# Row maxima of attention scores by key differences: half of the evictions moved to ScalarE, the rest fused on VectorE

## The chip, the cores and the metric

One Trainium2 chip; the kernel runs on one of its cores. The metric is device microseconds of one execution, the median of several. Engines: PE is TensorE (matmuls), PEld its weight loads, DVE is VectorE, ACT is ScalarE, POOL is GpSimd, SP is SyncE, which here only issues transfers.

## The reference

Three stages in a row: attention with pooled queries, a soft mixture of experts, and a two-layer network with a quadratic step.

```python
# q, k, v: (4, 8, 1152, 64); the queries are averaged in pairs
q_pool = q.reshape(B, H, S // 2, 2, D).mean(axis=3)            # 576 queries
scores = scale * q_pool @ k.transpose(0, 1, 3, 2)              # 576 x 1152 for each of 32 heads
scores = scores - np.max(scores, axis=-1, keepdims=True)       # the row maxima
attn = np.exp(scores); attn = attn / (attn.sum(-1, keepdims=True) + 1e-9)
x = (attn @ v).transpose(0, 2, 1, 3).reshape(2304, 512)
# mixture: logits = x @ phi (32 slots), softmax over tokens, two layers for each expert,
#          then softmax over slots and back to 2304 x 512
# network: h = x @ w_in; g = h if h >= 1, 0 if h <= -1, else (h + 1)**2 / 4; out = g @ w_out
```

## The kernel before

**Attention, two heads at a time.** There are 16 pairs of heads (`P`), and for each pair 9 chunks of 128 keys (`c`), so 144 steps `g = 9 P + c`. Each step has two halves, one for each head (`h`). In a half, TensorE works in this order: a part of the row maxima of a later pair (`max_half`), the transposed scores of this step (`st`), and the product of the step before with the values (`pv`). The maxima run `LEAD = 11` steps ahead of the scores that use them, so pair 0's maxima come in a lead-in before step 0, and pair 1's are pressed into steps 0 to 6 (`P1G`), two of them in each of the steps 0 and 1.

**Row maxima.** For each of 9 groups `t` of 128 queries (from both heads) the products with all 1152 keys are formed, in two parts `a` of 2 x 288 keys. `K1` holds the keys in fp16 as a rounded part and its remainder, one below the other on the partitions, and `q1` the rounded queries twice, so that one matmul gives both products. Each part goes to a PSUM buffer of the ring `sc` (3 buffers, tag `sc`), and VectorE takes the maximum over its 576 columns (L332), into `mp[P][:, t, a]`. For three groups at a time of pair 0 (`RT`), ScalarE copies the first part to fp16 instead (L327), and VectorE takes the maxima of the copies in halves (`max_rt`, L342). `max_fin` takes the larger of the two columns and puts it, scaled, beside the queries' remainder in `qn2`; that tile is transposed into `q2`. The scores are then a second matmul with `q2` and `S2`, whose rows hold the rounded keys and a constant row for the maximum: the maximum is subtracted in the matmul.

**The ring.** Score tiles (`st`), maxima tiles and the tiles of `t_x` share the 3 buffers of `sc`. A maxima tile reuses the buffer of the score tile two halves before, and a score tile that of the maxima tile one half before: a late eviction holds up TensorE.

**After the scores.** ScalarE takes the exp of a score tile (L407) into `E`, a ring of 4 + 3 SBUF buffers (`e`, `e2`). The sums over keys are made by first adding tiles: VectorE adds chunks 1, 2, 3 and 5 to chunk 0 (`es_add`, L415, by the list `ADD`), after GpSimd has added chunk 4 into 3 and 7 into 6 (`ge_add`, L420, by `GAD`). Then matmuls with a column of ones sum over the partitions (`es_sum`, L430), one block of matmuls for each group of `GRP`: before, three blocks (the added-up tile, 6 with 7, and 8).

**Between pairs.** At step 0 of the next pair TensorE does a transposing product for the pair before the last one (`t_x`, L479) and the row sums (`es_sum`); ScalarE copies results (`t_raw` L448, `t_sum` L456, `t_ev` L483) and scales tokens (`t_mul` L492, at places from the list `TML`); VectorE makes the divisors (`t_fin`, L460 to L464). Every fourth pair a softmax over the tokens of a batch is added.

**The order of the work is written out by hand.** `at(g, slot, f)` puts a call into a half-step; the lists `PREP` (loads, rounding and transposes of a later pair's keys and queries: `prep_khi`, `prep_klo`, `prep_qp`, `prep_qhi`, `prep_qlo`, `xpose_k`, `xpose_q1`), `CVS` and `CVL` (places of the weight conversion) hold such places. In a half-step's slot the calls come behind the matmuls of that half. All transfers are issued by SyncE, in program order.

**Weight conversion.** Sixteen pieces of the last layer's weights are loaded as pairs of 32-bit words and turned into floats: `cv_load`, `cv_abs` (ScalarE, L203), four `cv_step` (VectorE, L210 to L218), `cv_move` (to DRAM). Before, eleven pieces run in pairs 1 to 14, four steps each at step 0, and five in pair 15. The rest of the weights is converted in the last stage.

**Behind attention** come the mixture (weights of 1 MB each, loaded ahead piece by piece) and the network, whose matmuls (L1050) fill the last 220 us. The change doesn't touch their work.

Of the kernel before, what the change touches and what calls it, by code (L numbers as in the profile page):

```python
# [11 lines left out]
I32 = mybir.dt.int32  # L12
# [8 lines left out]
FILL = 38, 2, 8, 5  # L21
# [13 lines left out]
ADD = (((4, 1, 0, 0, 2), (6, 1, 1, 0, 2), (7, 2, 0, 0, 2), (8, 2, 1, 0, 2), (11, 3, 0, 0, 2), (12, 3, 1, 0, 2),  # L35
        (14, 5, 0, 0, 2), (15, 5, 1, 0, 2)),
       tuple((2 * c + h + 2, c, h, 0, 2) for c in range(1, 7) for h in range(2)))

PREP = (-20, -18, (-34, -33), -36, -16, -30), (-24, -21, (-36, -35), -37, -17, -31)
# [3 lines left out]
def fused_kernel(ctx: ExitStack, tc: tile.TileContext, q, k, v, phi, w1, w2, w_in, w_out, out):  # L43
# [60 lines left out]
    f64b = [cst([128, DM, 2], f"f64_{i}", I32) for i in range(2)]  # L104
# [76 lines left out]
    sq = xf[:, 1952:1952 + 2 * SW]  # L181

# [123 lines left out]
    def s2_fill(P):  # L306
        nc.sync.dma_start(out=S2b[P % 2][0:64], in_=K1[P][0:64])

    def max_half(P, t, a):
        if t == 0 and a == 0:  # L310
            mp[P] = g2.tile([128, NK, 2], F32, tag="mp", name=f"mp{P}")
# [12 lines left out]
        rt = RT[P] if P < len(RT) else ()  # L324
        if rt and a == 0 and rt[0] <= t < rt[-1]:

            nc.scalar.activation(out=mcp[:, t].rearrange("p (i n) -> p i n", i=2), in_=ps[:, :, 0:HQ], func=AF.Copy,  # L327
                                 scale=1.0 / MS)
            if t + 1 in rt:
                max_rt(P, rt[rt.index(t + 1) - 1], t + 1)  # L330
            return
        nc.vector.tensor_reduce(out=mp[P][:, t, a:a + 1], in_=ps[:, :, 0:HQ], op=ALU.max, axis=AX.XY)  # L332
        if mc:
            mc.pop(0)()

    mc = []
    mcp = xl.bitcast(F16)[:, 0:NK * TQ].rearrange("p (t n) -> p t n", t=NK)

    def max_rt(P, t0, t1):
        x, n, o = mcp[:, t0:t1], HQ, mp[P][:, t0:t1, 0]  # L340
        while n > HQ // 8:
# [872 lines left out]
```

## Time and profile before

| | |
|---|---|
| median of 3 runs | 739.67 us (738.88 to 740.59) |
| the profiled execution | 738.26 us, span 736.5 us |
| TensorE busy | 720.2 us, 98% of the span |
| VectorE busy | 587.4 us, 80% |
| ScalarE busy | 462.5 us, 63% |
| GpSimd busy | 221.4 us, 30% |
| granted TensorE clock | 1.00 throughout |

The span is what the profile covers, and the run's own time has 1.8 us around it. Times in rows are microseconds from the span's start unless marked ns. "idle before <-X" says how long the engine had been idle and what ended that.

### The profile page before, as it was taken

The page shows a single profiled execution, that of the slowest core. Times are in us where ns is not written, and L with a number is a line of the kernel's source. Part 1 is how long each engine was busy: PE and PEld are TensorE (multiplying, and loading weights), DVE is VectorE, ACT ScalarE, POOL GpSimd, SP SyncE. Part 2 cuts the span into 40 slices and gives each one's busy share as a digit, 9 for nine tenths or more (in the row PEclk, how much of TensorE's full clock was granted, in tenths as well). Part 3 has the DMA queues.
Part 4 walks back from the last instruction along what each step waited for, and adds up shares of the span by engine and source line. Part 5 has one row for each costly group of instructions (what it writes and reads, how often), then busy time and mean ns, then how long its engine had stood idle before and what let it go on. Part 6 is the DMA issues. An engine that isn't in the chain of part 4 may idle for free.

```text
span 736.5 us, 19455 instructions
## 1 busy us (share of the span) xinstructions
PE 720.2 (98%) x8017; PEld 563.8 (77%) x8017; DVE 587.4 (80%) x993; ACT 462.5 (63%) x881; POOL 221.4 (30%) x197
## 2 busy tenths in 40 slices
PE   8799999999999999999999999999999999999998
PEld 8677787877787877777877776536888888888887
DVE  5999999989999989999989758524667898896552
ACT  4355667757667757667766668314797677667640
POOL 6221132132132232232232232012533244424350
PEclk9999999999999999999999999999999999999999
DMA  9699789886878986877975619897102121200122
GB/s 211 147 226 222 164 204 214 189 195 148 163 216 196 189 204 143 191 198 187 200 189 132 217 35 294 323 416 312 58 1 86 61 83 58 87 28 1 72 86 101
DMA packets 130649, 118.75 MB, mean 161 GB/s; under 512 B 81152, under 2 KB 99840, under 8 KB 128512
## 3 DMA queue, kind: packets, MB, share of 16 engines
q1 hardware_dynamic: 130560, 117.50, 60.1%
q8 instruction: 63, 1.03, 0.6%
q14 instruction: 26, 0.21, 0.1%
HBM read 82.90 MB, written 8.91 MB: 125 GB/s over the span
## 4 chain that ended last, share of the span: by engine, by line
PE 86%; DVE 7%; issue 3%; DMA 2%; ACT 2%; SPq 0%; DVEq 0%; ACTq 0%
PE po L1050 26%; PE st L402 18%; PE acc L437 16%; PE mx L318 8%; PE tx L479 4%; PE acc L430 3%; DVE mp L332 3%; PE h L980 2%; PE s2o L851 2%; PE h L794 2%; DVE es L415 1%; ACT e L407 1%; DMA f<-in_moe_w_out_dram 1%; PE po L1056 1%; DMA kf<-in_k_dram 1%
## 5 line engine op out<-in xcount | busy, mean ns | idle before, releaser
L407 ACT ACTIVATE e<-st 128x576 f32<-128x576 f32 x288 | 187.5, 651 | 101.9 <-PE st L402 95.5
L332 DVE TENSOR_REDUCE mp<-mx 128x1 f32<-128x576 f32 x282 | 210.3, 748 | 27.9 <-PE mx L318 24.7
L437 PE MATMUL acc<-e,vf 128*64 128x288 f32 x1152 | 198.9, 408 | 1.7 <-ACT e L407 1.7
L402 PE MATMUL st<-q,K 128*64 128x288 f16 x1152 | 128.5, 288 | 3.9 <-DVE mp L332 2.4
L318 PE MATMUL mx<-K,q 128*64 128x288 f16 x1152 | 124.2, 286 | 4.8 <-DVE mp L332 2.7
L402 PE MATMUL st<-q,S 128*64 128x288 f16 x1152 | 128.5, 286 | 0.0
L420 POOL TENSOR_TENSOR e<-e,e 128x576 f32<-128x576 f32 x60 | 88.7, 1499 | 132.4 <-PE acc L437 126.2
L318 PEld LDWEIGHTS <-q 128*64 128x64 f16 x1152 | 76.1, 110 | 55.3 <-issue 6.0
L1019 POOL TENSOR_TENSOR glo<-r,ghi 128x1024 fp32r<-128x1024 f32 x34 | 81.9, 2408 | 114.5 <-DVE r L1007 74.2
L1050 PE MATMUL po<-whi,ghi 128*128 128x512 f32 x280 | 109.8, 392 | 0.0
L1050 PE MATMUL po<-wlo,ghi 128*128 128x512 f32 x280 | 109.6, 391 | 0.0
L1050 PE MATMUL po<-whi,glo 128*128 128x512 f32 x280 | 109.4, 391 | 0.0
L402 PEld LDWEIGHTS <-K 128*64 128x64 f16 x1152 | 74.2, 109 | 24.2 <-issue 13.1
L437 PEld LDWEIGHTS acc<-e,vf 128*64 128x64 f32 x1152 | 82.2, 137 | 8.3 <-issue 4.0
L415 DVE TENSOR_TENSOR es<-es,e 128x576 f32<-128x576 f32 x100 | 84.2, 843 | 0.0
L402 PEld LDWEIGHTS <-S 128*64 128x64 f16 x1152 | 75.6, 110 | 1.0 <-issue 0.2
L1062 DVE TENSOR_TENSOR pa<-po,pa 128x512 f32<-128x512 f32 (+1 forms) x54 | 36.8, 681 | 39.8 <-PE po L1050 39.7
L1050 PEld LDWEIGHTS po<-whi,glo 128*128 128x128 f32 x280 | 52.6, 188 | 12.0 <-POOL glo L1019 0.3
L1050 PEld LDWEIGHTS po<-whi,ghi 128*128 128x128 f32 x280 | 52.6, 188 | 10.9 <-issue 0.4
L1050 PEld LDWEIGHTS po<-wlo,ghi 128*128 128x128 f32 x280 | 52.6, 188 | 10.1
L1007 DVE SCALAR_TENSOR_TENSOR r<-h,cl 128x512 f32<-128x512 f32 x68 | 43.6, 681 | 7.6 <-ACT cl L1003 4.1
L492 ACT ACTIVATE xl<-xl,ss 128x96 f32<-128x96 f32 x150 | 47.1, 366 | 0.0
(204 smaller groups left out, 877.6 us busy)
## 6 DMA issues: line engine op xcount, KB each, us to landing
w<-in_moe_w_dram SPq DMA_DIRECT2D x76, 256.0 KB, 4.0
w<-in_moe_w_dram SPq DMA_DIRECT2D x12, 1024.0 KB, 12.3
vf<-in_v_dram SPq DMA_DIRECT2D x16, 576.0 KB, 4.2
kf<-in_k_dram SPq DMA_DIRECT2D x30, 288.0 KB, 5.0
f<-in_moe_w_in_dram SPq DMA_DIRECT2D x16, 512.0 KB, 4.9
f<-in_moe_w_out_dram SPq DMA_DIRECT2D x16, 512.0 KB, 3.5
qf<-in_q_dram SPq DMA_DIRECT2D x30, 256.0 KB, 5.8
S<-K SPq DMA_DIRECT2D x16, 288.0 KB, 4.6
```

Source lines behind the costliest of these rows:

```text
L318: nc.tensor.matmul(ps[p0:p1, i, 0:HQ], lhsT=q1[P][:, t, p0:p1], rhs=kk[:, j * HQ:(j + 1) * HQ], start=True, stop=True)
L332: nc.vector.tensor_reduce(out=mp[P][:, t, a:a + 1], in_=ps[:, :, 0:HQ], op=ALU.max, axis=AX.XY)
L402: nc.tensor.matmul(ps[c0:c0 + 64, i, 0:HQ], lhsT=kk[:, ci, c0:c0 + 64], rhs=f[:, sl[i]], start=first, stop=not first)
L407: nc.scalar.activation(out=e, in_=ps[:, :, 0:HQ], func=AF.Exp, scale=ESC)
L415: nc.vector.tensor_tensor(out=Es[P, n, h][:, i0:i1], in0=a[:, i0:i1], in1=b[:, i0:i1], op=ALU.add)
L420: nc.gpsimd.tensor_tensor(out=E[P, c, h], in0=E[P, c, h], in1=E[P, c + 1, h], op=ALU.add)
L437: nc.tensor.matmul(acc[P, i][h * 64:(h + 1) * 64, 0:HQ], lhsT=vt[P][:, h, c, :], rhs=E[P, c, h][:, i, :], start=(c == 0), stop=(c == NK - ...
L492: nc.scalar.activation(out=x, in_=x, func=AF.Copy, scale=ss[P][:, h, t:t + 1])
L1007: nc.vector.scalar_tensor_tensor(out=r[:, a:a + 2], in0=ps[a // 2], scalar=-1.0, in1=cl[:, a:a + 2], op0=ALU.max, op1=ALU.add)
L1019: nc.gpsimd.tensor_tensor(out=glo[k], in0=r, in1=ghi[k].bitcast(F32), op=ALU.subtract)
L1050: nc.tensor.matmul(ps, lhsT=a, rhs=b, start=st_, stop=sp)
L1062: nc.vector.tensor_tensor(out=t, in0=po, in1=t, op=ALU.add)
```

## The change

The maximum of two products a and b is a + max(b - a, 0). The changed kernel uses it for the two halves of a head's keys. VectorE forms the differences of the keys once a pair (`k_diff`: second half less first half, in fp16, into `KD`). The first part of each group's maxima is then the product with the differences; ScalarE evicts it as its positive part (Relu) into `RW`, an SBUF tile with two buffers. The second part is the product with the first half of the keys; VectorE adds the positive parts to it and takes the maximum in the same instruction (`tensor_tensor_reduce`), straight into `mp`. The matmuls stay as many. The copies of pair 0 (`RT`, `max_rt`) and the small maximum in `max_fin` are gone. Around that:

- GpSimd's adds (`ge_add`) are gone; VectorE adds chunks 1 to 7 to chunk 0 (14 adds a pair instead of 8), and there are two blocks of row sums in a pair instead of three, but for the last pair, which is as before. The ring `e2` has 4 buffers instead of 3.
- The weight conversion runs at one piece a pair, at fixed places, and each load is issued behind the piece before it, into one buffer instead of two.
- There is one `S2` instead of two, filled in two parts: chunks 0 to 4 four steps before the pair, the others at its step 0.
- The places of the preparation (`PREP`), of `t_mul` (`TML`) and of the adds are new; `prep_qhi`, for one, moves from the pair's step 1 to step 0. Pair 0 has fewer fill matmuls (`FILL`).

```diff
-FILL = 38, 2, 8, 5
+FILL = 38, 1, 8, 5
-RT = (0, 3, 6),
-CVS = ((0, 0),) * 4, ((0, 0),) * 4, ()
-CVL = 4, 6
+CVS = (10, 12, 17, 18, 20), (8, 9, 10, 11, 12)
+CVL = 1
-TML = (3, 0, 0), (3, 0, 1), (4, 1, 0), (4, 1, 1), (5, 0, 2), (5, 0, 3), (6, 1, 2), (6, 1, 3), (7, 0, 4), (7, 1, 4)
+TML = (2, 0, 0), (2, 0, 1), (3, 1, 0), (4, 1, 1), (4, 0, 2), (6, 0, 3), (6, 1, 2), (7, 1, 3), (7, 0, 4), (7, 1, 4)
-GRP = ((0, 1, 2, 3, 4, 5), (6, 7), (8,)), ((0, 1, 2, 3, 4, 5, 6), (7,), (8,))
-GAD = (10, 3, 0), (11, 3, 1), (16, 6, 0), (17, 6, 1)
+GRP = ((0, 1, 2, 3, 4, 5, 6, 7), (8,)), ((0, 1, 2, 3, 4, 5, 6), (7,), (8,))
-PREP = (-20, -18, (-34, -33), -36, -16, -30), (-24, -21, (-36, -35), -37, -17, -31)
+PREP = (-20, (-36, -35), (-34, -33), (-34, -33), -36, -32, -32, -30), (-24, (-42, -40), (-37, -37), (-35, -34), -38, -36, -34, -31)
+KDS = -26, -19
...
-    def s2_fill(P):
-        nc.sync.dma_start(out=S2b[P % 2][0:64], in_=K1[P][0:64])
+    def s2_fill(P, c0, c1):
+        o, i = [x[0:64].rearrange("p (h c) k -> p h c k", h=2)[:, :, c0:c1] for x in (S2, K1[P])]
+        nc.sync.dma_start(out=o, in_=i)
+
+    def key_half(P, h):
+        return K1[P][:, h * NK:(h + 1) * NK, :].rearrange("p c k -> p (c k)")
+
+    def k_diff(P, h):
+        kk = key_half(P, h)
+        nc.vector.tensor_tensor(out=KD[:, h], in0=kk[:, TQ:2 * TQ], in1=kk[:, 0:TQ], op=ALU.subtract)
...
-                kk = K1[P][:, h * NK:(h + 1) * NK, :].rearrange("p c k -> p (c k)")
-                j = 2 * a + i
-                nc.tensor.matmul(ps[p0:p1, i, 0:HQ], lhsT=q1[P][:, t, p0:p1], rhs=kk[:, j * HQ:(j + 1) * HQ],
+                kk = key_half(P, h) if a else KD[:, h]
+                nc.tensor.matmul(ps[p0:p1, i, 0:HQ], lhsT=q1[P][:, t, p0:p1], rhs=kk[:, i * HQ:(i + 1) * HQ],
                                  start=True, stop=True)
-        if P == 0:
+        if P == 0 and a == 0:
...
-        nc.vector.tensor_reduce(out=mp[P][:, t, a:a + 1], in_=ps[:, :, 0:HQ], op=ALU.max, axis=AX.XY)
+        if a == 0:
+            nc.scalar.activation(out=RW[:, t % 2], in_=ps[:, :, 0:HQ], func=AF.Relu)
+        else:
+            r = RW[:, t % 2]
+            nc.vector.tensor_tensor_reduce(out=r, in0=ps[:, :, 0:HQ], in1=r, scale=1.0, scalar=-3.0e38, op0=ALU.add, op1=ALU.max,
+                                           accum_out=mp[P][:, t:t + 1])
...
-            at(b - 9 if P > 1 else 1, 1, s2_fill, P)
+            at(b - 4, 0, s2_fill, P, 0, 5)
+            at(b, 0, s2_fill, P, 5, NK)
...
         for n in range(16):
-            g, sl = cvs[0]
-            at(*divmod(2 * g + sl - 1, 2), cv_abs, n)
+            ab, *st_ = [2 * NK * n + x for x in CVS[n // 15]]
+            at(*divmod(ab, 2), cv_abs, n)
             for i in range(4):
-                g, sl = cvs.pop(0)
-                at(g, sl, cv_step, n, i)
+                at(*divmod(st_[i], 2), cv_step, n, i)
+            if n < 15:
+                at(*divmod(st_[3] + 1, 2), cv_load, n + 1)
```

## Rows read from the trace of the kernel before

**Rows 1.** The page: busy time of each engine.

```profile
PE 720.2 (98%) x8017; PEld 563.8 (77%) x8017; DVE 587.4 (80%) x993; ACT 462.5 (63%) x881; POOL 221.4 (30%) x197
```

**Rows 2.** The page: the chain that ended last, by engine.

```profile
PE 86%; DVE 7%; issue 3%; DMA 2%; ACT 2%; SPq 0%; DVEq 0%; ACTq 0%
```

**Rows 3.** Windows, one pair: length, then busy us of PE, PEld, DVE, ACT, POOL.

```profile
core 0: us, PE busy (x) PEld busy (x) DVE busy (x) ACT busy (x) POOL busy (x), PEclk, DMA share, GB/s
239.00:265.60 26.60, 26.41 (x389) 21.16 (x385) 25.23 (x40) 18.76 (x39) 7.34 (x8) 1.00 0.91 199
```

**Rows 4.** Timeline at a pair's boundary, then the longest gap: start, length, engine.

```profile
247.77 0.69 DVE L218 SCALAR_TENSOR_TENSOR wst<-f,wst 128x512 int32<-128x512 int32 x1
...
248.32 0.41 ACT L448 ACTIVATE xT<-acc 128x288 f32<-128x288 f32 x1 [1.22 <-PE acc L437]
...
248.63 0.30 ACT L456 ACTIVATE es<-acc 128x160 f32<-128x160 f32 x1
...
249.33 0.41 PE L318 MATMUL mx<-K,q 128*64 128x288 f16 x4
...
250.55 0.41 PE L318 MATMUL mx<-K,q 128*64 128x288 f16 x4
250.57 0.50 DVE L460 STREAM_TRANSPOSE xT<-es 128x320 f32<-128x320 f32 x1
...
250.79 0.41 PE L402 MATMUL st<-q,K 128*64 128x288 f16 x4
250.88 0.67 ACT L289 ACTIVATE qn<-qf 128x576 f16<-128x576 f32 x1
...
251.44 1.53 DVE L332 TENSOR_REDUCE mp<-mx 128x1 f32<-128x576 f32 x2
...
252.19 0.44 PE L402 MATMUL st<-q,K 128*64 128x288 f16 x4
...
263.88 0.44 PE L402 MATMUL st<-q,K 128*64 128x288 f16 x4 [0.17 <-DVE mp L332]
```

**Rows 5.** Groups by form: line, engine, shapes, count | busy us, mean ns | idle.

```profile
L332 DVE TENSOR_REDUCE mp<-mx 128x1 f32<-128x576 f32 x282 | 210.3, 748 | 27.9 <-PE mx L318 24.7
...
L407 ACT ACTIVATE e<-st 128x576 f32<-128x576 f32 x288 | 187.5, 651 | 101.9 <-PE st L402 95.5 <-DVE es L415 1.7 <-ACT e L407 0.3
...
L492 ACT ACTIVATE xl<-xl,ss 128x96 f32<-128x96 f32 x150 | 47.1, 366 | 0.0
...
L430 PE MATMUL acc<-e,cols 128*32 128x160 f32 x512 | 20.3, 299 | 0.0
...
L367 DVE TENSOR_SCALAR qn<-mm 128x9 f16<-128x9 f32 x16 | 3.0, 189 | 0.6
```

**Rows 6.** Timeline, pairs 0 and 1 (SP, DVE and PE, each by itself).

```profile
27.57 0.59 SPq L253 DMA_DIRECT2D qf<-in_q_dram  x1
...
31.18 0.76 DVE L286 TENSOR_TENSOR qf<-qf 128x576 f32<-128x576 f32 x1
31.86 2.74 DVE L332 TENSOR_REDUCE mp<-mx 128x1 f32<-128x576 f32 x4
...
33.81 0.68 PE L437 MATMUL acc<-e,vf 128*64 128x288 f32 x4
...
50.58 0.68 PE L437 MATMUL acc<-e,vf 128*64 128x288 f32 x4
```

**Rows 7.** Two lines of VectorE: min/median/max ns, first and last start.

```profile
L286 DVE TENSOR_TENSOR qf<-qf x15: 746/1698/1708, 6.7 to 378.9; 128x576 f32<-128x576 f32 x15
...
L415 DVE TENSOR_TENSOR es<-es,e x100: 740/748/1955, 42.0 to 458.8; 128x576 f32<-128x576 f32 x100
```

**Rows 8.** Timeline of the last pair, PE and ACT.

```profile
438.22 0.41 PE L402 MATMUL st<-q,K 128*64 128x288 f16 x4
...
441.77 1.84 PE L479 MATMUL tx<-tab,xT 128*32 128x192 f32 x48
...
452.71 0.66 ACT L203 ACTIVATE wst<-f 128x512 f32<-128x512 f32 x1 [1.39 <-DMA f<-in_moe_w_out_dram]
...
460.56 0.75 PE L430 MATMUL acc<-es,cols 128*32 128x160 f32 x16
```

More of the change, by code (lines that the diff above doesn't have):

```diff
@@ L103, in fused_kernel @@
     wst = [cst([128, DM], f"wst{i}") for i in range(2)]
-    f64b = [cst([128, DM, 2], f"f64_{i}", I32) for i in range(2)]
+    f64b = [cst([128, DM, 2], "f64_0", I32)]
     NWL = NWA + NW0
@@ L169, in fused_kernel @@
     tab = g4.tile([128, HPB, 2, BW], F32, name="tab")
-    mx1 = g4.tile([128, NS], F32, name="mx1")
-    dg = g4.tile([128, NS], F32, name="dg")
-    S2b = [pr_p[i].tile([128, 2 * NK, 128], F16, name=f"S2_{i}") for i in range(2)]
+    S2 = gk.tile([128, 2 * NK, 128], F16, name="S2")
+    KD = g2.tile([128, 2, TQ], F16, name="KD")
+    RW = g2.tile([128, 2, 2, HQ], F32, name="RW")
     qn2b = [g2.tile([128, NK, 128], F16, name=f"qn2_{i}") for i in range(2)]
@@ L195, in cv_load @@
             src = w_out[r0:r0 + 128, :]
-        nc.sync.dma_start(out=f64b[n % 2], in_=src.rearrange("p (f t) -> p f t", t=2))
-        cv[n] = f64b[n % 2], None, (x + 8 if 12 <= n < 16 else x - 4) if x >= 4 else 4 + 4 * (qd % 2) + x
+        t = f64b[n % 2 if n >= 16 else 0]
+        nc.sync.dma_start(out=t, in_=src.rearrange("p (f t) -> p f t", t=2))
+        cv[n] = t, None, (x + 8 if 12 <= n < 16 else x - 4) if x >= 4 else 4 + 4 * (qd % 2) + x
     def cv_abs(n):
@@ L323, in max_half @@
                     nc.tensor.matmul(fl[0][p0:p0 + 64, 0:HQ], lhsT=q1[P][:, t, p0:p0 + 64], rhs=kk[:, 0:HQ], start=True, stop=True)
[L324 to L331, printed above, removed]
-        nc.vector.tensor_reduce(out=mp[P][:, t, a:a + 1], in_=ps[:, :, 0:HQ], op=ALU.max, axis=AX.XY)
[L333 to L341, printed above, removed]
-            mc.append(lambda n=n: nc.vector.tensor_tensor(out=x[:, :, 0:n], in0=x[:, :, 0:n], in1=x[:, :, n:2 * n], op=ALU.max))
-            n //= 2
-        mc.append(lambda: nc.vector.tensor_reduce(out=o, in_=x[:, :, 0:2 * n], op=ALU.max, axis=AX.X))
+        if a == 0:
[4 more added lines that the diff above has]
+                                           accum_out=mp[P][:, t:t + 1])
     fl = {}
@@ L354, in max_fin @@
     def max_fin(P):
[L355 to L365 removed]
         qn2 = qn2b[P % 2]
[L367 removed]
+        nc.vector.tensor_scalar(out=qn2[:, :, D], in0=mp[P], scalar1=-1.0 / MS, scalar2=None, op0=ALU.mult)
         if P == 0:
@@ L397, in st @@
         sl = [slice(h * TQ + i * HQ, h * TQ + (i + 1) * HQ) for i in range(2)]
-        for kk, f, first in ((K1[P], f1, True), (S2b[P % 2], f2, False)):
+        for kk, f, first in ((K1[P], f1, True), (S2, f2, False)):
             for i in range(2):
@@ L403, in st @@
                                      start=first, stop=not first)
-        ep, et, en = (g2, "e2", 3) if P < NP - 1 and (2 * (NK * P + c) + h) % 7 > 3 else (g3, "e", 4)
+        ep, et, en = (g2, "e2", 4) if P < NP - 1 and (2 * (NK * P + c) + h) % 8 > 3 else (g3, "e", 4)
         e = ep.tile([128, 2, HQ], F32, tag=et, bufs=en, name=f"e{P}_{c}_{h}")
@@ L415, in es_add @@
         nc.vector.tensor_tensor(out=Es[P, n, h][:, i0:i1], in0=a[:, i0:i1], in1=b[:, i0:i1], op=ALU.add)
-    def ge_add(P, c, h):
-        nc.gpsimd.tensor_tensor(out=E[P, c, h], in0=E[P, c, h], in1=E[P, c + 1, h], op=ALU.add)
     def es_sum(P):
@@ L617, in plan @@
             at(b - 8, 1, load_v, P)
-            at(b - 9 if P > 1 else 1, 1, s2_fill, P)
+            at(b - 4, 0, s2_fill, P, 0, 5)
+            at(b, 0, s2_fill, P, 5, NK)
         last = P == NP - 1
-        for s, *a in () if last else GAD:
-            at(b + s // 2, s % 2, ge_add, P, *a)
         for s, *a in ADD[last]:
@@ L665, in fused_kernel @@
         fill(FILL[0])
+        nc.vector.memset(S2[64:128], 0.0)
+        nc.gpsimd.memset(S2[64:65], MS)
         for i in range(2):
-            nc.vector.memset(S2b[i][64:128], 0.0)
-        for i in range(2):
-            nc.gpsimd.memset(S2b[i][64:65], MS)
             nc.gpsimd.memset(qn2b[i][:, :, D:2 * D], 0.0)
@@ L697, in fused_kernel @@
                 at(g, i, *x)
+        at(-9, 1, k_diff, 0, 1)
         at(-3, 1, prep_qlo, 1)
-        for n in range(2):
-            at(CVL[n], 1, cv_load, n)
+        at(-3, 1, k_diff, 1, 0)
+        at(0, 1, k_diff, 1, 1)
+        at(CVL, 1, cv_load, 0)
         def tab_fill():
```

53 lines of the change are left out of this document (22 added, 31 removed).

## Prediction

> **What bounds the kernel now.** I read the page's busy times first: TensorE is busy 720.2 of 736.5 us, VectorE 587.4, ScalarE 462.5 [rows 1]. The chain that ended last says the same: 86% of it runs through TensorE, 7% through VectorE [rows 2]. Then the windows, one stretch for each pair of heads: a pair without the softmax extras takes 26.60 us, with VectorE busy 25.23 us (95%), ScalarE 18.76 us (71%), GpSimd 7.34 us [rows 3]. So this stage has two limits close together: TensorE's own work, and VectorE, which must empty a PSUM buffer every half-step. The timeline shows how they mix. One half-step (maxima, scores, values) takes 249.33 to 250.55, 1.22 us, when nobody is late [rows 4]. Where VectorE is late the score matmuls start late: they should follow at 250.79 + 1.22 = 252.01 and start at 252.19. From there to the next boundary I count seven such gaps, the first this one and the longest the one in front of 263.88, whose row names VectorE's reduction; they add up to **1.1 us a pair**. The view of waits shows little of it, because the modelled ends of matmuls cover such gaps.
>
> **What is added and removed, by engine, for one pair (9 steps).**
>
> TensorE. The matmuls for maxima stay 8 per step. What goes is one of three blocks of the row sums (`es_sum`): the group of chunks 6 and 7 is now added up elsewhere. The 512 instructions of the form with `e` are 32 blocks of 16 and take 20.3 us, so 0.63 us a block [rows 5]; 15 pairs lose one: **-9.5 us**. TensorE has no cover for that block (it sits alone at the pair's boundary), so it counts in full.
>
> VectorE. 18 reductions of 0.748 us go [rows 5], each costing about 0.67 of the queue, since the next one starts before the last has ended (four in 2.74 us at 31.86 [rows 6]). Nine fused instructions come. The trace holds none. From below: the same 576 columns in one pass cost 0.748 (reduction) and as much for an add that nothing disturbs (median 748 [rows 7]). From above: the fused one also writes a column of maxima, and the nearest small write of VectorE takes 0.189 [rows 5], so 0.94 if that is a full instruction behind the pass. I take 0.80 of queue (0.67 and two thirds of a small write), as nothing says that the whole start of an instruction is paid again.
> The Trainium skill (VectorE: DVE Perf Modes, section Two Vector instructions with no wait between them) says that an operation which also writes out its accumulator is two instructions, the main one and an accumulator read; that speaks against the change. The trace of before has no such operation; by that rule the price would sit at the upper end, 0.94, and if half of the 1.3 us that this adds to VectorE's pair turned into waits, the sum below would end at 739 instead of 730.
> GpSimd's four adds a pair go, and the adds of `es` on VectorE rise from 8 to 14, 6 x 0.67 = 4.0 us. Two key differences come, each between 0.19 (a small instruction) and 0.75 (an add of this width); I take 0.45, so 0.9 us. One small instruction, the maximum of the two columns, goes, 0.2. And GpSimd's adds no longer disturb VectorE: the add of the query pairs takes 0.746 at best and 1.698 in the median, and an `es` add up to 1.955 against a median of 0.748 [rows 7]: about 1.1 us back.
> The Trainium skill (SBUF — State Buffer, section Who interferes with whom) says a VectorE instruction with two SBUF inputs contends with a GpSimd instruction that reads SBUF; the trace agrees, with that 0.746 against 1.698.
> Sum for VectorE: 25.2 - 12.1 + 9 x 0.80 + 4.0 + 0.9 - 0.2 - 1.1 = 23.9 us a pair, against a pair of about 26: 92%, little relief. With the fused instruction at 0.94 it is 25.2.
>
> ScalarE. Nine evictions of 128x576 come. The exp of the same shape from PSUM takes 651 ns [rows 5] and starts the next one 0.1 earlier (a copy 0.41 long at 248.32, the next at 248.63 [rows 4]), so 0.55 each, 5.0 us: 18.8 to 23.7 us a pair. Each now holds a PSUM buffer that TensorE needs a half-step later, in a queue that carries everything else of ScalarE.
>
> **Where that queue is late.** I lay the changed order over the boundary of [rows 4], with 248.32 as zero. ScalarE there: copy of the accumulator 0, its sums 0.31, then the rounding of the queries, which the new plan moves here from a later slot (0.67 long at 250.88 before), at 0.61, exp at 1.2, copy 1.75, sums 2.05, and only then the positive part at 2.35, done at 3.0. Its matmul is done at 249.33 + 0.41, i.e. 1.4, and the scores of the next half-step, at 250.79 or 2.47, need that buffer: late by 0.5 us. VectorE behind it: the transpose of sums waits for ScalarE until 2.35, its three instructions take 250.57 to 251.44, 0.87; then comes a step of the weight conversion, now placed here, 0.69 (the row at 247.77); then the fused maximum, done at 4.7. The scores due at 2.47 + 0.5 + 1.22 = 4.2 wait 0.5. At step 3 the plan puts three scalings (47.1 us for 150, 0.31 each [rows 5]) into one slot, in front of the next positive part: some 0.4 more. That is 1.4 us a pair against the 1.1 of before: 13 pairs, **+4 us**. Queued behind the late positive part are the exp of the same half-step and the scalings, and for these TensorE waits only a step later. The other slots fit: steps 5 to 7 hold 2.2 to 2.3 us of ScalarE's work for 2.44.
>
> **The last pair.** Before, five of the sixteen conversions of weights run here, each with a load issued just ahead. The row at 452.71 shows ScalarE idle 1.39 us on such a load, with the exps queued behind it [rows 8]. From 438.22 to the row sums at 460.56 there are 17 half-steps without maxima, 0.98 us each (1.22 less the 0.24 from 250.55 to 250.79 [rows 4]), and one block of 1.84: 18.5 us. The stretch takes 22.3, so 3.8 are lost. The new plan spreads the conversions one to a pair and leaves one here, its load issued about 6 us ahead of its first reader. I count **-3 us** and leave 0.8 for that load.
>
> **The start.** With half of the maxima on ScalarE the lead-in over pair 0 ends sooner, but pair 2's queries, whose last piece is issued at 27.57, are added by VectorE at 31.18 right as they land, and this add stands in front of pair 1's fused maxima. Nothing moves that load, so most of the lead is waited away. From 33.81 to 50.58 twelve half-steps take 16.77 us instead of 14.6 [rows 6], with VectorE as the limit through pair 1's doubled maxima; most comes back: **-1.6 us**. Fewer fill matmuls are inside that.
>
> What costs nothing: the key differences' order (two and more steps ahead of their first matmul), the split copy into the one `S2` (issued four steps ahead, and five steps ahead for its second part), and one load buffer for weights instead of two (a conversion a pair). They are hidden by these distances; without them each would cost a transfer's latency a pair. SyncE's queue stops at the `S2` copy until TensorE has passed chunk 4, which delays what stands behind it by less than a step.
>
> **Sum.** -9.5 + 4 - 3 - 1.6 = about -10 us on the profiled span of 736.5, whose run took 738.26; the median of the three runs is 739.67, so **730 us**.
>
> **Rivals.**
> - *VectorE becomes the bound.* It ends on the other side. With the fused instruction at T, VectorE's load is 16.7 + 9T; at 95% use, as now, a pair takes (16.7 + 9T)/0.95. With 4.6 us gained at the ends (0.33 a pair over 14), the kernel is no faster once that reaches 26.9, at T = 1.0 us. At 1.1 a pair takes 28.0: +20 - 4.6, 755 us; at twice the pass, 1.34, it takes 30.3, and the kernel some 787. For it: a fused instruction with a second output is not in the trace, and VectorE stands at 95%. Against: one pass over 576 columns is 0.75 for every form here. Chance 0.16.
> - *ScalarE's queue costs more than I laid out*: 2.4 us a pair instead of 1.4. Then +17 - 9.5 - 4.6, 742 to 745. For it: 91% use and strict order. Against: the steps without extras have 0.3 to 0.5 us spare. Chance 0.13.
> - *The evictions run free.* If VectorE's one deadline a step (not two) removes the waits of 1.1 us a pair, leaving 0.3: -9.5 - 11 - 4.6, 715. Chance 0.15.
> - *It cancels*: the saved block is taken up by later waits at the boundary, 736 to 741. Chance 0.09.
> - The forecast, 723 to 736: 0.47.
>
> A change of 0.2% (1.5 us) is about what this measurement can tell from none. Faster: 0.47 + 0.15 + 0.03 of the cancelling case, 0.65. Same: the rest of that case, 0.06. Slower: the first two rivals, 0.29. The forecast's own range is 723 to 736; for 8 in 10 it must take in the free case nearly whole and the ScalarE case, but only the near part of the VectorE case: 715 to 748.
>
> **What would show it.** Right: the fused instruction at 0.75 to 0.9 us; row-sum instructions of the `e` form falling from 512 to 272; pairs of 25.9 to 26.3 us, with ScalarE near 90%; score matmuls late once or twice just behind each boundary, released by ScalarE; no idle of ScalarE on a weight load in the last pair. Wrong: a fused instruction of 1 us and more with VectorE above 95%, waits of TensorE on ScalarE in every step, or pairs without gaps.

## The result and the profile after

The changed kernel takes **730.22 us** (median of 4 runs, 729.23 to 730.49), against 739.33 us for the kernel before in the same rounds: ratio 0.9872, 95% interval 0.9855 to 0.9889. The prediction was 730. The profiled execution has a span of 727.5 us, 9.0 below the 736.5 of before.

The page's busy line, and the chain that ended last by engine, which answer to [rows 1, 2]:

```profile
PE 706.6 (97%) x7723; PEld 556.1 (76%) x7723; DVE 546.1 (75%) x1095; ACT 532.4 (73%) x1019; POOL 135.4 (19%) x136
...
PE 74%; ACT 10%; DVE 7%; issue 3%; DMA 3%; SPq 1%; POOL 0%; ACTq 0%; DVEq 0%; POOLq 0%
```

The work has moved as the diff says: TensorE has 13.6 us less, ScalarE 70 us more, GpSimd 86 us less. The chain now runs through ScalarE for 10% of the span.

The groups by line of the changed kernel (busy us, mean ns of one; then idle time before):

```profile
L394 DVE TENSOR_TENSOR es<-es,e 128x576 f32<-128x576 f32 x190 | 142.6, 759 | 6.6 <-ACT e L386 2.7
L333 DVE CUSTOM_DVE_ANT_0 RW<-mx,RW 128x576 f32<-128x576 f32 x144 | 108.4, 755 | 31.8 <-ACT e L386 19.8 <-PE mx L323 7.2 <-ACT RW L330 3.0
L330 ACT ACTIVATE RW<-mx 128x576 f32<-128x576 f32 x144 | 94.2, 656 | 12.2 <-PE mx L323 7.6 <-DVE mp L333 0.3
L313 DVE TENSOR_TENSOR KD<-K 128x576 f16<-128x576 f16 x32 | 14.5, 452 | 1.4 <-DMA K<-kn 1.4
L406 PE MATMUL acc<-e,cols 128*32 128x160 f32 x272 | 12.2, 299 | 0.0
L333 DVE DVE_READ_ACCUMULATOR2_ANT mp<- 128x1 f32 x144 | 12.0, 83 | 0.0
L284 DVE TENSOR_TENSOR qf<-qf 128x576 f32<-128x576 f32 x15 | 11.3, 751 | 2.2 <-DMA qf<-in_q_dram 2.2
```

The fused instruction is two rows, as wide a pass as the reduction was (755 ns against 748, [rows 5]) and a read of the accumulator of 83 ns. The row sums of the form with `e` fall from 20.3 us [rows 5] to 12.2: 8.1 us for 15 blocks, 0.54 each. The add of the query pairs, 1698 ns in the median before [rows 7], has a mean of 751.

Two windows of the changed kernel, a part of the lead-in and one ordinary pair from boundary to boundary (busy time of each engine, then clock, DMA share, GB/s); the second answers to [rows 3]:

```profile
12.30:26.00 13.70, 10.50 (x103) 7.89 (x100) 7.42 (x21) 7.70 (x13) 5.19 (x8) 0.88 0.95 215
...
239.67:265.80 26.13, 25.65 (x370) 20.82 (x368) 22.73 (x47) 23.20 (x48) 1.79 (x4) 1.00 0.86 209
```

The pair takes 26.13 us instead of 26.60, with VectorE at 87% and ScalarE at 89%.

The timeline of the changed kernel from just ahead of a boundary (its transposing product starts at 239.67) into step 3, answering to [rows 4]; it shows what ScalarE and VectorE do there, and the score matmuls that wait for them:

```profile
237.07 0.75 DVE L284 TENSOR_TENSOR qf<-qf 128x576 f32<-128x576 f32 x1
...
243.77 0.68 ACT L287 ACTIVATE qn<-qf 128x576 f16<-128x576 f32 x1
...
244.28 0.41 PE L323 MATMUL mx<-KD,q 128*64 128x288 f16 x4
244.34 0.65 ACT L386 ACTIVATE e<-st 128x576 f32<-128x576 f32 x1
...
245.34 0.68 ACT L330 ACTIVATE RW<-mx 128x576 f32<-128x576 f32 x1
...
245.54 0.44 PE L323 MATMUL mx<-K,q 128*64 128x288 f16 x4
...
246.08 0.44 PE L381 MATMUL st<-q,K 128*64 128x288 f16 x4
...
246.41 0.63 DVE L218 SCALAR_TENSOR_TENSOR wst<-f,wst 128x512 int32<-128x512 int32 x1
...
246.95 0.75 DVE L333 CUSTOM_DVE_ANT_0 RW<-mx,RW 128x576 f32<-128x576 f32 x1
247.05 0.44 PE L323 MATMUL mx<-KD,q 128*64 128x288 f16 x4
...
247.63 0.08 DVE L333 DVE_READ_ACCUMULATOR2_ANT mp<- 128x1 f32 x1
247.63 1.42 DVE L394 TENSOR_TENSOR es<-e,e 128x576 f32<-128x576 f32 x2
...
247.76 0.44 PE L381 MATMUL st<-q,K 128*64 128x288 f16 x4 [0.27 <-DVE mp L333]
...
252.69 0.90 ACT L468 ACTIVATE xl<-xl,ss 128x96 f32<-128x96 f32 x3
253.49 0.63 ACT L330 ACTIVATE RW<-mx 128x576 f32<-128x576 f32 x1
```

When nobody is late, scores start 0.24 to 0.25 us behind the maxima of their half-step. Here the maxima at 245.54 are followed by scores at 246.08, 0.29 late: the positive part they wait for ran from 245.34, behind the rounding of the queries at 243.77. Those of 247.05 are followed at 247.76, 0.47 late: the fused maximum of 246.95 stands behind the divisors and the conversion's fourth step. At step 3 three scalings stand in front of the positive part of 253.49, and scores start 0.31 late (253.62 to 254.17). With two of 0.05 these make 1.17 us a pair.

**Where the 9.0 us came from**, from the starts of the transposing products. The first is 2.45 us earlier (79.57 against 82.02); one dropped block lies ahead of it, so the start gave 1.91. Nine ordinary pairs give 3.60 together and three pairs with the softmax over a batch's tokens 0.08 (29.17, 29.53, 28.97 us against 29.19, 29.32, 29.24). Pair 14 gives 0.53, the block behind it 0.54, and the last pair 1.80. The mixture and the network are as before. All of these are differences of two profiled executions, and the start is the least certain of them (experiment 6).

### The profile page after: what moved, and what is told of

Same layout as the page of the kernel before. It is cut to its first block, busy times and chain, and to the rows that moved or that the text cites. A ratio compares the mean times of both kernels' runs of the same rounds, so it can differ in the third digit from the quotient of the medians.

```text
span 727.5 us, 19242 instructions
## 1 busy us (share of the span) xinstructions
PE 706.6 (97%) x7723; PEld 556.1 (76%) x7723; DVE 546.1 (75%) x1095; ACT 532.4 (73%) x1019; POOL 135.4 (19%) x136
## 4 chain that ended last, share of the span: by engine, by line
PE 74%; ACT 10%; DVE 7%; issue 3%; DMA 3%; SPq 1%; POOL 0%; ACTq 0%; DVEq 0%; POOLq 0%
PE po L1033 26%; PE st L381 14%; PE acc L413 13%; PE mx L323 5%; PE tx L455 3%; ACT xl L468 3%; ACT e L386 3%; ACT RW L330 2%; PE h L963 2%; DVE RW L333 2%; PE acc L406 2%; PE h L776 2%; DMA Wst<-cv_dr 1%; PE s2o L833 1%; DMA qf<-in_q_dram 1%
## 5 line engine op out<-in xcount | busy, mean ns | idle before, releaser
L386 ACT ACTIVATE e<-st 128x576 f32<-128x576 f32 x288 | 188.4, 655 | 28.2 <-PE st L381 25.6
L394 DVE TENSOR_TENSOR es<-es,e 128x576 f32<-128x576 f32 x190 | 142.6, 759 | 6.6 <-ACT e L386 2.7
L333 DVE CUSTOM_DVE_ANT_0 RW<-mx,RW 128x576 f32<-128x576 f32 x144 | 108.4, 755 | 31.8 <-ACT e L386 19.8
L330 ACT ACTIVATE RW<-mx 128x576 f32<-128x576 f32 x144 | 94.2, 656 | 12.2 <-PE mx L323 7.6
L381 PEld LDWEIGHTS <-K 128*64 128x64 f16 x1152 | 75.7, 109 | 23.2 <-issue 18.1
L323 PE MATMUL mx<-KD,q 128*64 128x288 f16 x576 | 63.0, 287 | 3.2 <-DVE KD L313 1.5
L323 PE MATMUL mx<-K,q 128*64 128x288 f16 x576 | 63.3, 288 | 2.2 <-ACT RW L330 2.1
L505 POOL TENSOR_TENSOR xT<-xT,xl 128x128 f32<-128x128 f32 x22 | 11.2, 510 | 233.9 <-ACT xl L468 233.9
```

Source lines behind the costliest of these rows:

```text
L330: nc.scalar.activation(out=RW[:, t % 2], in_=ps[:, :, 0:HQ], func=AF.Relu)
L333: nc.vector.tensor_tensor_reduce(out=r, in0=ps[:, :, 0:HQ], in1=r, scale=1.0, scalar=-3.0e38, op0=ALU.add, op1=ALU.max, accum_out=mp[P][:, ...
L381: nc.tensor.matmul(ps[c0:c0 + 64, i, 0:HQ], lhsT=kk[:, ci, c0:c0 + 64], rhs=f[:, sl[i]], start=first, stop=not first)
L386: nc.scalar.activation(out=e, in_=ps[:, :, 0:HQ], func=AF.Exp, scale=ESC)
L394: nc.vector.tensor_tensor(out=Es[P, n, h][:, i0:i1], in0=a[:, i0:i1], in1=b[:, i0:i1], op=ALU.add)
```

## Experiments

In each, the named kernel with only the edit shown. A pair's length is the distance between two transposing products.

**1. Is it the dropped block, or the relief of the evictions?** Three blocks again, with the adds of before.

```diff
-GRP = ((0, 1, 2, 3, 4, 5, 6, 7), (8,)), ...
+GRP = ((0, 1, 2, 3, 4, 5), (6, 7), (8,)), ...
+GAD = (10, 3, 0), (11, 3, 1), (16, 6, 0), (17, 6, 1)   # adds on GpSimd: 4 into 3, 7 into 6
-ADD = 14 adds on VectorE
+ADD = 8 adds on VectorE, the list of before
```

> The changed kernel with its fused maxima, but the row sums in three blocks again (chunks 4 and 7 added up by GpSimd, eight adds on VectorE). Theory (the time comes from the dropped block on TensorE): 15 blocks of 0.54 us come back, +8 us, and VectorE, 4 us a pair lighter, gives at most 0.3 us a pair of it back: 734 to 738 us, still below the 739.3 of before by the start and the last pair. Rival (the gain is the relief of the evictions): within 2 us of the changed kernel, 729 to 732 us.

Measured: 748.49 us, ratio to before 1.0114 (1.0094 to 1.0134). Neither theory: with the fused maxima and the old sums the kernel is *slower* than before, and 18 us above the changed one. A pair takes 27.67 us. The window of such a pair, and then its end in the timeline:

```profile
222.65:250.32 27.67, 26.62 (x387) 21.72 (x385) 20.60 (x41) 23.29 (x47) 8.08 (x8) 1.00 0.76 191
```

```profile
246.61 3.64 POOL L400 TENSOR_TENSOR e<-e,e 128x576 f32<-128x576 f32 x2 [4.84 <-PE acc L417]
...
247.01 1.97 DVE L285 TENSOR_TENSOR qf<-qf 128x576 f32<-128x576 f32 x1
248.90 0.74 DVE L334 CUSTOM_DVE_ANT_0 RW<-mx,RW 128x576 f32<-128x576 f32 x1
...
249.71 0.44 PE L382 MATMUL st<-q,K 128*64 128x288 f16 x4 [0.45 <-DVE mp L334]
```

VectorE is busy for only 74% of this pair, less than in the changed kernel. But the add of the query pairs runs beside GpSimd's adds and takes 1.97 us, where it takes 0.75 in the changed kernel (237.07). The fused maximum queues behind it, and the scores behind that start 0.72 us late (248.75 to 249.71). Earlier in the pair two adds, the first beside GpSimd's, take 1.89 us (241.16) where two take 1.42 in the changed kernel, and the scores behind them are 0.32 late instead of 0.05. The key differences are longer too, 648 ns in the mean against 452. The fused instruction itself is not (755 in both): it has one input in PSUM.

**2. The block alone, and GpSimd alone.** First a third block without any add on GpSimd:

```diff
-GRP = ((0, 1, 2, 3, 4, 5, 6, 7), (8,)), ...
+GRP = ((0, 1, 2, 3, 4, 5, 6), (7,), (8,)), ...
-       ... (15, 6, 1, 0, 2), (17, 7, 0, 0, 2), (17, 7, 1, 0, 2)),
+       ... (15, 6, 1, 0, 2)),
```

> The changed kernel with chunk 7 taken out of the added-up tile: a third block of row sums on TensorE, two adds a pair less on VectorE, and no add on GpSimd. The run with three blocks and GpSimd's adds took 748.5 us, 18 us above the changed kernel, where I had expected 8. Theory (the block is worth 0.54 us a pair in full, and the other 10 us come from VectorE's work beside GpSimd's adds): 15 x 0.54 = 8 us, less at most 3 us for the lighter VectorE: 735 to 738.5 us. Rival (the third block itself costs more at the boundary than its matmuls, because VectorE and ScalarE are late there): 743 us or more.

Measured: 736.78 us, ratio 0.9968 (0.9956 to 0.9980), 6.6 us above the changed kernel. Ordinary pairs take 26.68 us, 0.54 more than 26.14, which is the block's own length to the hundredth; two adds less on VectorE give nothing back in them. The block counts in full, as predicted. The two runs with three blocks differ by 11 to 12 us, 0.99 of it in each ordinary pair; that much comes with GpSimd's adds, though the adds left on VectorE are fewer there too (8 instead of 12) and stand in other slots. This kernel, with the fused maxima and three blocks, is also 0.3% faster than before.

Then two blocks, with one add a head given to GpSimd:

```diff
-ADD: (9, 3, 0, 0, 2), (8, 3, 1, 0, 2), (11, 4, 0, 0, 2), (10, 4, 1, 0, 2)
+ADD: (12, 3, 0, 0, 2), (13, 3, 1, 0, 2)
+ge_add of 4 into 3 at slots 10 and 11
```

> The changed kernel, two blocks, with one add a head and pair (chunk 4 into 3) on GpSimd instead of VectorE. VectorE has 1.3 us a pair less to do; TensorE's work is the same. Theory (GpSimd's adds slow VectorE's instructions beside them, and TensorE waits for that): slower than the changed kernel by 2 to 6 us, 732 to 736 us, with longer key differences or adds of the query pairs. Rival (a lighter VectorE is a gain wherever the add runs): 726 to 729.5 us.

Measured: 736.50 us, ratio 0.9964 (0.9952 to 0.9977), at the upper end of the theory's range and slightly past it. A pair takes 26.59 us, though VectorE is a microsecond lighter (21.73). The timeline of this kernel:

```profile
258.72 2.79 POOL L399 TENSOR_TENSOR e<-e,e 128x576 f32<-128x576 f32 x2 [1.11 <-PE acc L416]
...
260.91 2.08 DVE L394 TENSOR_TENSOR es<-es,e 128x576 f32<-128x576 f32 x2
262.90 0.42 DVE L210 TENSOR_SCALAR wst<-wst 128x512 f32<-128x512 f32 x1
263.24 0.75 DVE L333 CUSTOM_DVE_ANT_0 RW<-mx,RW 128x576 f32<-128x576 f32 x1
...
264.05 0.44 PE L381 MATMUL st<-q,K 128*64 128x288 f16 x4 [0.31 <-DVE mp L333]
```

Two adds take 2.08 us, where two take 1.42 in the changed kernel (247.63). The first of them, begun while GpSimd was still adding, took 1.21 us. The fused maximum behind them is late, and the scores wait 0.51 us (263.30 to 264.05) in a place where those of the changed kernel wait 0.05. The two adds also stand in other slots than in the changed kernel, so the run doesn't separate the two altogether; but the disturbed add is 0.46 us longer than the others (754 ns in the median), and without that the wait would be 0.05 here too.

**3. Do the adds need the fused maxima?** The kernel before with the new groups and adds:

```diff
-GRP, GAD, ADD of before
+GRP = ((0, 1, 2, 3, 4, 5, 6, 7), (8,)), ...;  GAD = ();  ADD = 14 adds on VectorE
```

> The kernel before with its plain maxima (18 reductions a pair on VectorE), and the row sums in two blocks with all 14 adds on VectorE. Theory (the fused maxima make the room for the adds): VectorE's 25.2 us a pair become about 28 to 29 and bound the pair, 27.9 us and more instead of 26.6: 755 to 775 us, although TensorE has 8 us less to do. Rival (the adds would have fitted without the fused maxima): 731 to 735 us.

Measured: 764.43 us, ratio 1.0326 (1.0306 to 1.0347). Ordinary pairs take 28.6 us, and a stretch of 28 us shows VectorE busy for 27.45, 98%. So the two blocks with plain maxima cost 25 us. The rest of the change with the sums of before costs 9 (experiment 1), but saves some 2 with three blocks and no add on GpSimd (experiment 2), and with two blocks it saves 9.

**4. Is it the conversion?** The kernel before with the conversion's places of the changed one (`CVS`, `CVL`, one load buffer).

> The kernel before with nothing changed but the places of the weight conversion: one piece a pair with one load buffer, as in the changed kernel. Theory: the last pair gives back about 2 us, and five conversions more inside the pairs, 2.8 us of VectorE each, cost about as much or more: 737 to 745 us. Rival (the conversion's places are a main part of the gain): 734 us or less.

Measured: 746.35 us, ratio 1.0092 (1.0072 to 1.0111), a little past the theory's range. Its stretch through the last pair, between the last two transposing products, takes 19.86 us instead of 21.96, 2.1 less. So the conversion's places alone account for the last pair's gain. But ordinary pairs take 27.25 us instead of 26.6, although each has one conversion as before: VectorE is busy for 24.7 us of such a pair (25.2 before), and the scores are late by 1.75 us in it instead of 1.1. The conversion's steps now stand in front of reductions: behind a step of 0.41 us (242.10) scores are 0.45 late, where the same scores were 0.11 late before. What the spread is worth beside the fused maxima was not run by itself.

**5. The clock in the lead-in.**

```diff
-FILL = 38, 1, 8, 5
+FILL = 38, 2, 8, 5
```

> The changed kernel with two fill matmuls a partition half in the lead-in instead of one. The granted clock from 12.3 to 26.0 us is 0.88 in the changed kernel. Theory: the lead-in waits for ScalarE and for the last piece of the queries anyway, so a full clock there gives 0 to 0.6 us: 729.6 to 730.4 us. Rival (the lower clock hid more of the gain): 728.5 us or less.

Measured: 730.60 us, ratio 0.9873 (0.9852 to 0.9894): no change. The granted clock between 12.3 and 26.0 us is 1.00 here against 0.88. The first scores start at 28.25 instead of 29.72, but nothing of that is left at the first transposing product, which starts at 79.57 in both. That the fill sets the clock is not shown: two later kernels with two fill matmuls (`qhi_earlier` and `conv4_halfstep` below) have 0.89 and 0.88 in the same window. In the changed kernel the clock is 0.50 from 22 to 24 us, and ahead of that TensorE had stood idle, waiting for a positive part:

```profile
21.01 0.44 PE L323 MATMUL mx<-K,q 128*64 128x288 f16 x4 [2.08 <-ACT RW L330]
```

**6. The three predicted waits, taken away one at a time.** The first two tries moved the work to a place that was free by its engine, and both made the kernel slower.

```diff
-PREP[1]: query rounding -36, its transpose -34, remainder -31; dup_q1 at b - 15
+PREP[1]: query rounding -31, its transpose -30, remainder -30; dup_q1 at b - 14
```

> The changed kernel with the rounding of the queries moved off the pair's boundary to slot 5 of the pair, where ScalarE has nothing extra (its transpose and what reads it a slot behind). Theory (it delays the positive part behind it, and the scores start 0.29 us late for that): 13 pairs x 0.3 = 4 us less, 726 to 727.5 us. Rival (the wait only moves, as the next one ends later on VectorE): 729.5 to 731 us.

```diff
-CVS = (10, 12, 17, 18, 20), (8, 9, 10, 11, 12)
+CVS = (12, 13, 17, 18, 24), (8, 9, 10, 11, 12)      # piece 14 keeps its places
```

> The changed kernel with the fourth step of each weight conversion moved from behind the divisors (step 1 of the pair) to step 3, where VectorE has only the fused maximum. Theory (conversion step and divisors together make the fused maximum late, and the scores wait 0.47 us): 14 pairs x 0.3 to 0.47 = 4 to 6.5 us less, 724 to 726.5 us. Rival (the divisors alone are late enough, since they wait for ScalarE's copies): 729 to 731 us.

Measured: 734.30 us (0.9934, 0.9922 to 0.9947) and 733.15 us (0.9917, 0.9904 to 0.9931). Neither theory nor rival holds in either. With the rounding moved, the 0.29 left its place, but 0.28 stood half a step earlier (246.76 to 247.28), the wait behind the divisors shrank to 0.26, and the wait behind the three scalings, with the rounding now two positive parts ahead of it on ScalarE, grew to 0.50: 1.2 us in the pair, as before the move. Besides, the copy of the transposed queries is now issued at 260.35, behind the loads of a later pair's keys and queries, and the next maxima wait for it. A row of TensorE's timeline, and a window of the lead-in of the same kernel:

```profile
263.27 0.44 PE L323 MATMUL mx<-KD,q 128*64 128x288 f16 x4 [0.56 <-DMA q<-q]
```

```profile
26.00:38.00 12.00, 8.30 (x86) 6.54 (x88) 6.75 (x15) 6.21 (x11) 0.00 (x0) 0.86 0.53 127
```

With the conversion moved, the 0.47 did go. But the next piece's load is issued behind the fourth step, here behind the loads of keys and queries too, and lands too late; ScalarE, and the exps behind it, stand still, and so does TensorE (timeline):

```profile
263.78 0.66 ACT L203 ACTIVATE wst<-f 128x512 f32<-128x512 f32 x1 [1.32 <-DMA f<-in_moe_w_in_dram]
...
265.03 0.46 PE L413 MATMUL acc<-e,vf 128*64 128x288 f32 x1 [0.99 <-ACT e L386]
```

Both also start the first pair's boundary 1.8 us later (81.32 and 81.38 against 79.57), and both have a granted clock of 0.86 between 26 and 38 us, where the changed kernel has 1.00. (The expectation of the next run names a later stretch for this; the rows say 26 to 38.) It is 0.50 from 34 to 37 us, and TensorE had stood idle ahead of that, for 2.44 us up to 32.43 in the first and 2.11 up to 32.65 in the second, until a fused maximum that stands behind the add of pair 2's queries. Neither edit touches what runs ahead of 38 us, so this goes with the execution and not with the move. At 47 us the scores are 1.0 and 1.2 us later than in the changed kernel. Most of what the first adds to that comes at 50.32, where the maxima of pair 2 wait 0.70 us for the copy that the edit issues later. The moves lost all the same: the nine ordinary pairs are 3.2 us longer together in either kernel.

So the moves were made again, by as little as would do, with two fill matmuls as in 5:

```diff
-PREP[1]: query rounding -36
+PREP[1]: query rounding -37
```

> The changed kernel with the rounding of the queries one slot earlier, ahead of the boundary's block (and two fill matmuls in the lead-in, which changed nothing by themselves: 730.6 us). Moving it later put its transpose and the copy behind it too late (a wait of 0.56 us on that transfer at 263.27, and the clock of the lead-in fell later, at 38 to 50 us). Earlier, ScalarE has about 1.1 us idle while TensorE does the transposing product. Theory (the rounding delays the positive part, and nothing else is late there): 0.29 us for each of 13 pairs: 726 to 728 us. Rival (the wait only passes on to the fused maximum one step later, which VectorE sets): 729.5 to 731 us.

```diff
-CVS = (10, 12, 17, 18, 20), (8, 9, 10, 11, 12)
+CVS = (11, 13, 17, 18, 21), (9, 10, 11, 12, 13)
```

> The changed kernel (with two fill matmuls) with the fourth step of each conversion half a step later, behind the fused maximum instead of in front of it, the next load half a step later with it, and its first steps half a step to a step later. Moving it four slots put that load too late (ScalarE idle 1.32 us on it, the exps behind it). Theory: the scores behind the divisors start 0.3 to 0.47 us sooner in 14 pairs: 724 to 727 us. Rival (the half-step's later load makes ScalarE wait, or the fused maximum was late for the divisors alone): 729.5 us or more.

```diff
-TML: ... (7, 1, 3), (7, 0, 4), (7, 1, 4);  lg_add at g0 + 3, 1
+TML: ... (7, 1, 3), (8, 0, 4), (8, 1, 4);  lg_add at g0 + 4, 1
```

> The changed kernel (with two fill matmuls) with two of the three scalings of slot 7 moved to slot 8, behind the positive part of that step. Theory (three scalings in front of the positive part make the scores 0.31 us late): 13 pairs x 0.3 = 4 us less: 726 to 727.5 us. Rival (the wait only moves on a step): 729.5 to 731 us.

Measured: 727.56 us (0.9836, 0.9822 to 0.9850), 726.81 us (0.9833, 0.9815 to 0.9851) and 729.65 us (0.9861, 0.9847 to 0.9876). The first two hold: ordinary pairs of 25.86 and 25.87 us against 26.14. (Their first boundaries stand at 80.91 and 80.36, so the whole kernel shows less of this than the pairs do.) The timeline of ScalarE with the rounding moved, first, and of VectorE with the conversion moved, second:

```profile
238.75 0.68 ACT L287 ACTIVATE qn<-qf 128x576 f16<-128x576 f32 x1
...
241.28 1.03 ACT L459 ACTIVATE xl<-tx 128x480 f32<-128x480 f32 x2 [0.78 <-PE tx L455]
```

```profile
245.58 0.75 DVE L333 CUSTOM_DVE_ANT_0 RW<-mx,RW 128x576 f32<-128x576 f32 x1
246.25 0.08 DVE L333 DVE_READ_ACCUMULATOR2_ANT mp<- 128x1 f32 x1
246.25 0.69 DVE L218 SCALAR_TENSOR_TENSOR wst<-f,wst 128x512 int32<-128x512 int32 x1
```

The rounding now stands ahead of the time in which ScalarE is idle for the transposing product (0.78 left), and the fused maximum ahead of the conversion step. The wait of 0.47 went, and further on in the pair one of 0.10 came and one of 0.05 grew to 0.15; the pair is 0.27 shorter. Of the third, the wait of 0.30 went too, but 0.13 came and 0.05 grew to 0.11 further on, and the pairs with the batch softmax became 0.33 us longer; its interval overlaps that of the changed kernel.

**7. Together.** The rounding at -37, the conversion of `conv4_halfstep`, one scaling moved instead of two, two fill matmuls, and:

```diff
+            c += 4 * (P == NP - 2)        # pair 14's scalings two steps later
             at(g0 + c // 2, c % 2, t_mul, P, h, t)
-        at(g0 + 3, 1, lg_add, P)
+        at(g0 + 4 + 2 * (P == NP - 2), 0, lg_add, P)
```

> The changed kernel with the moves that each gave something: the rounding of the queries one slot earlier (-0.28 us a pair), the conversion's fourth step half a step later (-0.27 us a pair), one scaling instead of two moved to slot 8 (up to -0.3 us a pair), two fill matmuls in the lead-in, and the scalings of pair 14 in the last pair two steps later, so that they don't run beside those of pair 13. Theory (the waits behind the boundary are separate and add up; the last pair's loss of 2 us is ScalarE's queue of scalings): ordinary pairs of 25.3 to 25.6 us, the last pair 1 to 1.5 us shorter, 720.5 to 724 us. Rival (one wait removed uncovers the next, so the moves don't add): ordinary pairs of 25.85 us, 726 us or more.

Measured: **719.07 us** (718.18 to 719.50), ratio 0.9718 (0.9695 to 0.9741), better than the theory's range. The page's busy line and the same place of a pair in TensorE's timeline:

```profile
PE 702.1 (98%) x7741; PEld 555.8 (77%) x7741; DVE 545.6 (76%) x1095; ACT 525.2 (73%) x1019; POOL 136.9 (19%) x136
```

```profile
241.60 0.44 PE L323 MATMUL mx<-K,q 128*64 128x288 f16 x4
241.87 0.44 PE L381 MATMUL st<-q,K 128*64 128x288 f16 x4
```

The scores follow their maxima at 0.27. Ordinary pairs take 25.34 us, 0.80 below the changed kernel, with 0.39 us of waits left; the pairs with a batch softmax 28.2 to 28.5. The last pair, from its transposing product to the next, takes 18.67 us instead of 20.17. The moves add up in the pairs (0.28 and 0.27 us by themselves, and 0.13 to 0.19 with two scalings moved), and the rival of one wait covering the next has fallen.

## Why the prediction was right

Step by step, forecast against measurement:

| step of the prediction | forecast | measured |
|---|---|---|
| one block of row sums less, 15 times, in full | -9.5 | -8.1 (0.54 each, not 0.63) |
| waits in the pairs, net | +4 | +2.8 |
| last pair | -3 | -1.8 |
| start | -1.6 | -1.9 |
| sum, on the span | -10 | -9.0 |

The mechanism was the forecast one, but that the time came out within 0.3 us of 730 is partly luck: the gains of the block and of the last pair were put too high by 1.4 and 1.2 us and the waits too high by 1.2, and these errors partly cancel.

- **The block.** Right in kind, and experiment 2 shows it without anything beside it: 26.68 against 26.14. The size was off because the group's busy time was shared out evenly. The timeline of the changed kernel has one block with `e` alone and, behind the last pair, two in a row:

```profile
429.82 0.73 PE L406 MATMUL acc<-e,cols 128*32 128x160 f32 x16
...
452.13 1.27 PE L406 MATMUL acc<-e,cols 128*32 128x160 f32 x32
```

One block takes 0.73 us and two take 1.27, so the second adds 0.54, and it was the second of two that fell away.
- **The waits.** All three places that were laid out from the order of the queues were found, at 0.29, 0.47 and 0.31 us where 0.5, 0.5 and 0.4 were forecast: with two of 0.05, 1.17 a pair, not 1.4. The +2.8 is what is left of the blocks' 8.1 after start and last pair are taken off: 8.1 + 1.9 + 1.8 - 9.0. It falls in two parts. The nine ordinary pairs lose 9 x 0.54 - 3.60 = 1.3 us. The three with the batch softmax lose 3 x 0.54 - 0.08 = 1.5. These pairs had no conversion before and have one now, which the prediction didn't price apart. That this is what takes their gain was not tested by itself: in experiment 4, where they also get one, they are 0.4 to 0.5 us longer, but the ordinary pairs, which had one before, are 0.65 longer.
- **The fused instruction.** 0.80 us of queue was forecast. The row at 246.95 is followed by the accumulator read at 247.63 and by the next add at the same moment: 0.68. Its bounds, 0.748 and 0.94, were both too high, since they were durations, and only the start-to-start time is paid. The Trainium skill (VectorE: DVE Perf Modes, section Two Vector instructions with no wait between them) says that such an operation is two instructions; the trace agrees, with a second row of 83 ns, but it shows no cost for it in the queue. The 739 us worked out by it did not come.
- **VectorE.** 23.9 us a pair was forecast and 22.73 is measured; the fused instruction explains 9 x 0.12 = 1.1 of it. ScalarE: 23.7 forecast, 23.20 measured.
- **GpSimd.** The prediction counted 1.1 us of VectorE's time for it and no time of the kernel. That term was mis-sized: in experiments 1 and 2 all of GpSimd's adds beside the fused maxima come with 11 to 12 us, and one add a head and pair with 6. Before, the same disturbance was there too [rows 7], and it cost time there as well, which the prediction didn't see. The longest of its seven gaps, the 0.36 us in front of 263.88, stands behind an add that ran beside GpSimd's (259.77 to 262.55). VectorE's timeline in the kernel before:

```profile
261.98 1.18 DVE L415 TENSOR_TENSOR es<-es,e 128x576 f32<-128x576 f32 x1
263.08 0.74 DVE L332 TENSOR_REDUCE mp<-mx 128x1 f32<-128x576 f32 x1
```

The add is 0.43 us longer than the others, and the reduction behind it is late by that. No run took GpSimd's adds out of the kernel before. The query add (1.70 us at 269.78) stood just ahead of the transposing product of 270.78 there, and no score needed the reduction behind it before that product was done; in experiment 1 it stands in front of a fused maximum, and the scores wait 0.72. The Trainium skill (SBUF — State Buffer, section Who interferes with whom) says that an instruction of VectorE with two SBUF inputs contends with a GpSimd instruction that reads SBUF. The runs agree: the query add goes from 0.75 to 1.97 us, while the fused instruction with its one SBUF input stays at 755 ns.
- **The start.** As laid out, the add of pair 2's queries waits for their load and stands in front of pair 1's fused maxima (30.18, then 30.98, in the changed kernel). But -1.9 is the value of one execution. In `conv4_later`, whose work is the same up to 38 us, the scores at 47 us are 1.2 us later, so that the forecast of -1.6 came this close is partly luck. Which part of the change gives the start its gain was not tested.
- **The last pair.** The wait on a weight load is gone, as forecast. What the forecast missed is what became late next: the scalings of two pairs meet there. The timeline of the changed kernel:

```profile
439.15 1.16 ACT L468 ACTIVATE xl<-xl,ss 128x96 f32<-128x96 f32 x4
...
440.75 1.16 ACT L468 ACTIVATE xl<-xl,ss 128x96 f32<-128x96 f32 x4
...
444.11 0.46 PE L413 MATMUL acc<-e,vf 128*64 128x288 f32 x1 [0.91 <-ACT e L386]
```

Eight scalings in two rows stand between the exps. With pair 14's moved two steps the same stretch is 1.5 us shorter (experiment 7). The conversion there also stood half a step later, which gives 0.3 by itself (19.86 us in `conv4_halfstep`).

- **The rivals.** VectorE as the bound needed 1.0 us for the fused instruction, and it is 0.68. ScalarE's queue at 2.4 us of waits a pair is 1.17. The evictions did not run free, but they nearly can: with the order mended, 0.39 us of waits a pair are left, and the kernel stands at 719, close to the 715 of that rival. The block was not taken up at the boundary either: the ordinary pairs keep 0.40 of its 0.54 us. The one `S2`, the larger ring `e2` and the new places of the preparation, which were to cost nothing, were not tried by themselves.

## What to carry to other kernels

An edit that loses alone can win beside another: the new sums with the old maxima cost 25 us, since VectorE was full, and with the fused maxima they save; so price a change by the engine that is left full at each stage, not edit by edit. The loss of the fused maxima with the old sums had another cause, GpSimd's adds, and only a run that took these out alone showed it. An engine's busy share alone doesn't say whether it holds the kernel up: a pair with VectorE at 74% was 1.0 us slower, beyond its extra block, than one at 87%, because two disturbed adds stood in front of evictions. When an instruction must leave a crowded place, move it by the smallest step that puts it behind (or into a gap ahead of) the eviction, and look at which transfers its place also sets: a conversion step moved four slots made the ordinary pairs 0.36 us longer in the mean, and moved half a step 0.22 shorter.

## What the runs showed of the hardware

- The read of the accumulator behind the fused instruction, 83 ns, costs the queue nothing: the next instruction starts at the same moment as it (247.63).
- The same VectorE add takes 0.75 us alone, 1.70 beside GpSimd's adds in the kernel before and 1.97 in experiment 1, and a key difference in fp16 648 ns in the mean against 452; the fused instruction, with one input in PSUM, is 755 ns in both.
- A granted clock of 0.88 over 13.7 us of the lead-in cost nothing that is left at the first boundary (79.57 with it and without, in one execution each). One of 0.86 over the 12 us from 26 to 38 stands with scores that are 1.0 and 1.2 us later at 47 us. Full is 2.4 GHz and the lower level 1.2, so each is a mean over a stretch that was partly at the lower one (0.50 from 22 to 24 us, and from 34 to 37). In all three traces TensorE had been idle ahead of the lower level, for 2.08, 2.44 and 2.11 us.
